# A new issue table for the first sixth of a written-out schedule, and a new origin for the array's first fill

## The chip, the cores and the metric

The kernel runs on one core of a Trainium2 chip. The metric is device time in microseconds; lower is better. Three runs of the kernel before took 366.05, 366.97 and 367.13 us; the median is 366.97 us. One further execution was profiled: it took 365.49 us in all, and its recorded span is 363.7 us.

## The reference, cut to what matters

The first half is a linear attention with a decaying state, for 4 batches, 8 heads, 768 steps and a head dimension of 48:

```python
for t in range(S):
    cur = einsum('bhd,bhe->bhde', u * kt, vt)
    y[:, :, t] = einsum('bhd,bhde->bhe', rt, state + cur)
    state = wt[..., None] * state + einsum('bhd,bhe->bhde', kt, vt)
```

The heads of y side by side give x, of shape (4, 768, 384). The second half is a gated network on it, all in float32:

```python
h = maximum(x @ w_in, 0)                     # 384 -> 1024
u, v = h[..., :512], h[..., 512:]
v_n = (v - mean(v)) / sqrt(var(v) + 1e-6)
v_s = einsum('ts,bsd->btd', w_spatial, v_n) + b_spatial
out = (u * v_s) @ w_out                      # 512 -> 384
```

## The kernel before, in words

**Tiling.** Time is cut in 24 slots of 128 steps (6 per batch). A slot loads its decays W, its keys and queries kr and its values v (L386 to L391), and DVE and POOL prepare them: products of neighbouring decays (L442), a step of k and r by single decays (L446), a scan backwards into F (L449), the floor of its end products (L451) and their reciprocal (L453), a scan forwards into E (L454), and k times F (L456), r times E (L460). TensorE then makes the scores paw (L525), the transposed keys KT (L543), the state's increments (L616) and the outputs py (L560). DVE masks the scores into AS (L529) and adds the increments into S (L629, L631). In the first six slots the bonus term with u goes over TensorE: rk (L414) times up_sb, a small copy of u, gives pg (L419), and bv (L491) is v times pg. The output y is evacuated on ACT and DVE (L663, L665), transposed (yt, L669) and split in a high and a low part (L673 to L679), since each large product is three matmuls of such parts (L686 to L688).

**The network.** hv_unit makes the v half (ph), its sum and sum of squares on ACT (L715 to L718). After every third slot a row of operations on 128x3 tiles named st (L735 to L743) makes mean and scale; L751 or L753 normalizes, L756 and L758 split into vh and vl. g_unit (pu, pv) and out_unit (po) follow for each half batch. The weights are taken in as 64-bit words and turned into float32 parts by integer operations (L354 to L361); the tiles d and e are named after the weight, ('wv', 0) being the first third of the v half of w_in. The spatial weights are split at L329 and L331.

**What sets the order.** Every operation is recorded with the engines it may run on, what it reads and writes, and its buffers. The string PLAN has one word for each of the 1930 operations: a letter for the engine (T is TensorE, V is DVE, A is ACT, G is POOL, S is SyncE's DMA queue) and a number in base 36, a start in hundredths of a microsecond. The operations are sorted by that number and issued:

```python
o.on, o.start = w[0], int(w[1:], 36) / 100
return sorted(self.ops, key=lambda o: o.start)
```

The number is used for the order alone (and for the fills below): each engine works through its own list in order, and an instruction starts when its semaphores allow it.

**Fills.** The function fill walks through the sorted list and, up to the slot FILL_TO, puts matmuls of a zero tile (zk, L893) in front of a TensorE operation wherever the table leaves over 0.3 us before it. How many is reckoned from a time t at which the array is taken to be free; up to COLD each is counted as 0.43 us, after it as 0.224 us. One fill is two records in the trace. TensorE runs them in order like everything else.

Of the kernel before, what the change touches and what calls it, by code (L numbers as in the profile page):

```python
# [18 lines left out]
G = H // 2  # L19
# [12 lines left out]
T2s S4g Tgq Aji Ajc S4x5 S5kl S6o Apg Vrs Vt1 Vxn Azp G12f Spf A1ph V1tz V1wl V1zy A221 G24f Sa0 A134 V15y  # L32
V178 V1al A1co V1kw S28 S3c S8w Vib Tkh Vbe Vk0 Vky Vcx Gf4 Vfy Vgm Vmu Goq A115 A14p Vcc Vzc Ts1 V11e Toz Ar1
T13o T15x Tx1 V10n A15e V1ej T18f A19v V1h2 T1s5 A1vc T1xl A23h Suq A1we V21n V2bl V2g0 A2qc G2xa Sng A1mu
V1r1 V1sa V1uw A2gd V2i8 S1h0 A2kw V2n4 V2pq V2sq A2us V345 S2v6 A3to G496 S238 A3gn V439 S25r A34s V38c S3xz
A4i8 V4r1 S4c7 A5nh V5qb S4ux A5gg V5ms S2sw A5tl G5yv S5jh A5uq V61n S1i4 A2o6 V2rf S5v7 A67e V6i0 S4jx A5af
V5hp S4y9 A5l7 V6jc S1je A2yj V31r V32u V363 A3d0 V5co S2i5 A3ju V3m4 V3q7 V4h2 A53l V5j1 S2qm A3m6 V4gb V4pq
V504 A5k2 V5o3 S4it V4wy V4zd V51f V55w A5mc V5rn T27w T29t T2e2 A2hs A2jk A2mh S5k S7s Sgo Vur Tyf Vlw Vwp
V1ca Vov Vwg V137 V13w Gzk G1f3 A1un A1ty Gfo V1d8 T1ke V1p8 A1fo T12s A1ax T1ov T1vv T1fr V1j8 A1kc V22l T1ym
A20y V23b T26n A28i T2bq A2ct T2j2 T2lj T2o5 A2t0 A2w8 A2wv Smc Sbd S1es V18w T1lv G1dh V1ml V1jy V1fd G1i1  # L40
V1iv V1nj G1o1 V1ya A29k A2a9 V24n T256 V2da A24j T1r9 A1sr T2c7 T2fz T23t V288 A2dv V302 T2ho A2ju V2ll T2ng
A2pa T2qv A2ry T2ts T2vp T2xm A305 A35x A36k A3bf G3xh V3lw G3x1 G3y9 G3z1 G3zt V40i V41z A457 V4cq A41g A43s
V45n A4aq A4e4 G4im S1do S1fw S224 V28y T2rc G22t G2di V2an V25z V27z V2f3 V2jw G2k5 V2o1 A343 A3aq V2x1 T39s
V3cs A388 T31e A32w T2zj T3jt T382 V3c1 A3e5 V3l0 T3l7 A3py V3s9 T3ur A3w1 T3yq A40e T44m T473 T490 A4cp A4fj
A4jd S1pg S210 S2j9 V2vd T3b9 V2uf V30t V37e V2yd V35u V39n V3ac G39w G3ed A3ut A3hs V3n7 T3i1 V3tl A3ng T3h5
A3in T3vf T41u T3ml V3rj G3ss V3ve T438 A46m V484 T4cs A4ft T4k1 A4l4 T4mp T4pa T4r7 A4ud A4w5 A4wt S2g8 S2lb
S3mk V3hf T3nz G3cr V3j3 V3k2 V3em G3l8 V3mu V3oj G3n3 G3u3 A4a1 V41h V3wv T40d V49f V40q T3qz A3sh T4ax T4dh
T3z7 V47c V4bz T4f7 A4h7 V4io T4ly A4n8 T4ot A4pw T4t4 T4v1 T4wy A4zh A51a A51x A54q V585 V55o G57g V58o V597
G59w V5av V5e0 A5hl V5l3 A5ei A5pt V5tc V5bf A5d2 V5fa T5nq S3rn A47o S4aj A4qy S4tt A56b S596 A5r8 T32a T33q
T36m A3by T5fy T5hy T5je T62h T65d T66t V69k V6ce A6ju G6m7 T356 T3e9 T3fp A3l4 T5ku T5ma T5o0 T5pg T5wo T5y4  # L50
V606 V658 A69o V6gp T3rv T3tb T3xa A3zc T63x T689 T69p T6fi T6l9 T6mp V6or V6qe A6s4 G6ui T4gl T4il T4ki A4tb
T5qw T5sc T5ts T5v8 T5zk T610 V63x V66k A68j V6kn T6rx T6td T6z5 T7aw V7cy S7fg T6w9 T6xp T7cc T7ds A7fu S8gi
T760 T780 T79g T7f8 A7ha S7tx T4yv T50b T537 A559 T6gx T6id T6jt T6o5 T6qh T6ut V6zd G73k A78b V7kw T51r T54n
T563 A58o T7go T7l0 T7mg T7pc T7sy T7ud V7wf V7y2 A89o V8ex T58f T59v T5bb A5j0 T85j T88w T8ac T8d8 T8eo T8g4
V8i6 G8k0 A8my V8pf T6b5 T6cl T6e1 A6g3 T7i4 T7jk T7nw T7rh T7vt T7x9 V7ze V84e A863 V87o T8hk T8j0 T8ro T8t4
A8v6 S945 T8bs T8q7 T8uk T8w0 A8y2 S931 T954 T9b5 T9cl T9e1 A9g3 S9hn S38s S3sr S5u3 S43x G47k V4fd V4ef V4k0
G4p2 V4sc V4t1 G4m7 V52r G683 V6b3 V6dq A6l8 A59q A6fn A6kz A6fe A6h5 A6ug T5eh V6xk T57k V59e V577 T70l T5cr
V5gy V5kc V5pf T72b A73r V759 T7qs A7t0 T87j A88m T8kg T8md T8oa A8qt A935 A93s S3lg S45b S6fh S4w1 G4v8 G4sl
# [60 lines left out]
Tqkl Tqrt Tqt9 Aqvb Sqwv Vn8u Tnlb Vp1v  # L119
"""  # L120

GAP, FILL_TO, COLD = 0.3, 5, 7.0

EARLY = 8

# [95 lines left out]
def kernel(  # L221
# [33 lines left out]
    op = prog.op  # L255
# [148 lines left out]
    def slot_prep(i):  # L404
# [490 lines left out]
    def fill(order):  # L895
        t = free = 1.1
# [152 lines left out]
```

## Time and profile before

| | |
|---|---|
| median of three runs | 366.97 us |
| profiled execution | 365.49 us |
| its span | 363.7 us |
| TensorE busy | 354.7 us (98%) |
| DVE busy | 279.1 us (77%) |
| ACT busy | 211.3 us (58%) |
| POOL busy | 138.0 us (38%) |
| loaded and stored by DMA | 47.81 MB |

The shares are means over the whole span. The first 65 us hold the preparation of the weights and the first six slots, the rest runs batch after batch; a share of one stretch is read from the view by stretches.

### The profile page before, as it was taken

How to read it: one execution, taken by the hardware profiler on the slowest of the kernel's cores; microseconds unless marked ns; L12 is line 12 of the kernel's file. 1: busy time of each engine (PE TensorE's matmuls, PEld its weight loads, DVE VectorE, ACT ScalarE, POOL GpSimd, SP SyncE). 2: the span in 40 equal slices, each digit the busy share in tenths (PEclk: the TensorE clock that was granted, in tenths of full speed). 3: DMA queues.
4: the chain of work that ended last, by engine and by line, in shares of the span. 5: the costliest groups of instructions: out<-in, count | busy, mean ns of one | idle time of the engine just before them, and what ended most of it. 6: DMA issues, size and time to landing. Idle time of an engine off the chain costs nothing.

```text
span 363.7 us, 11366 instructions
## 1 busy us (share of the span) xinstructions
PE 354.7 (98%) x4666; PEld 327.9 (90%) x4666; DVE 279.1 (77%) x591; ACT 211.3 (58%) x585; POOL 138.0 (38%) x182
## 2 busy tenths in 40 slices
PE   7998989999999999999999999999999999999997
PEld 6886787899998889799999999999999898899997
DVE  7999998798789998887999865878896876234330
ACT  2478887894555657773645588762464747621212
POOL 3344353412641755615632747132223514013220
DMA  7998546763265365731465445513463331000101
GB/s 205 287 275 231 158 115 174 223 201 98 75 183 167 95 189 179 199 99 43 122 181 166 129 135 162 159 45 112 120 184 96 124 120 45 0 23 0 49 20 69
DMA packets 21546, 47.81 MB, mean 131 GB/s; under 512 B 2545, under 2 KB 10354, under 8 KB 21490
## 3 DMA queue, kind: packets, MB, share of 16 engines
q1 hardware_dynamic: 21346, 46.85, 43.7%
q8 instruction: 37, 0.61, 0.7%
q10 hardware_dynamic: 144, 0.20, 0.1%
q14 instruction: 19, 0.16, 0.1%
HBM read 42.32 MB, written 4.72 MB: 129 GB/s over the span
## 4 chain that ended last, share of the span: by engine, by line
PE 78%; DVE 10%; ACT 6%; issue 2%; DMA 1%; POOL 1%; SPq 0%; DVEq 0%; ACTq 0%; POOLq 0%
PE pv L686 9%; PE pv L688 9%; PE pv L687 9%; PE py L560 5%; PE po L686 5%; PE po L687 4%; PE po L688 4%; PE ph L686 4%; PE ph L688 4%; PE ph L687 4%; PE pu L686 3%; PE pu L688 3%; PE pu L687 3%; PE py L893 3%; PE paw L525 2%
## 5 line engine op out<-in xcount | busy, mean ns | idle before, releaser
L686 PE MATMUL pv<-ws,vh 128*128 128x384 f32 x192 | 65.7, 342 | 0.3 <-ACT us L783 0.2
L688 PE MATMUL pv<-ws,vl 128*128 128x384 f32 x192 | 64.4, 335 | 0.0
L687 PE MATMUL pv<-ws,vh 128*128 128x384 f32 x192 | 64.3, 335 | 0.0
L792 DVE TENSOR_TENSOR t<-pv,b_sb 128x384 f32<-128x384 f32 x32 | 17.6, 552 | 26.7 <-PE pv L688 26.6
L686 PEld LDWEIGHTS pv<-ws,vh 128*128 128x128 f32 x192 | 36.0, 188 | 1.4 <-ACT us L783 0.9
L796 ACT CAST gh<-t 128x384 fp32r<-128x384 f32 x32 | 15.9, 512 | 36.7 <-DVE t L794 25.4
L687 PEld LDWEIGHTS pv<-ws,vh 128*128 128x128 f32 x192 | 36.1, 188 | 0.0
L688 PEld LDWEIGHTS pv<-ws,vl 128*128 128x128 f32 x192 | 36.0, 188 | 0.0
L686 PE MATMUL pu<-xT,wi 128*128 128x384 f32 x96 | 34.2, 357 | 0.0
L686 PE MATMUL po<-wo,gh 128*128 128x384 f32 x96 | 33.1, 345 | 0.0
L688 PE MATMUL pu<-xT,wi 128*128 128x384 f32 x96 | 32.5, 338 | 0.1
L687 PE MATMUL pu<-xT,wi 128*128 128x384 f32 x96 | 32.3, 336 | 0.0
L687 PE MATMUL po<-wo,gh 128*128 128x384 f32 x96 | 32.3, 336 | 0.0
L688 PE MATMUL po<-wo,gl 128*128 128x384 f32 x96 | 32.2, 335 | 0.0
L686 PE MATMUL ph<-wi,xT 128*128 128x512 f32 x72 | 30.6, 425 | 0.3 <-DVE t L792 0.3
L688 PE MATMUL ph<-wi,xT 128*128 128x512 f32 x72 | 28.5, 396 | 0.1
L687 PE MATMUL ph<-wi,xT 128*128 128x512 f32 x72 | 28.3, 393 | 0.0
L505 ACT ACTIVATE AS<-id,dgs 128x64 f32<-128x64 f32 x76 | 20.1, 337 | 6.1 <-DVE dgs L497 6.1
L456 POOL TENSOR_TENSOR kr<-kr,F 112x496 f32<-112x496 f32 x13 | 16.1, 1237 | 15.6 <-DVE kr L446 7.1
L446 POOL TENSOR_TENSOR kr<-kr,W 112x256 f32<-112x256 f32 x16 | 16.4, 1026 | 14.4 <-DMA kr<-in_tr_dram 11.5
L460 POOL TENSOR_TENSOR kr<-kr,E 112x512 f32<-112x512 f32 x13 | 16.2, 1245 | 14.0 <-DVE kr L446 5.8
L794 POOL TENSOR_TENSOR t<-t,us 128x384 f32<-128x384 f32 x9 | 9.6, 1067 | 31.1 <-DVE t L792 29.5
(199 smaller groups left out, 969.4 us busy)
## 6 DMA issues: line engine op xcount, KB each, us to landing
kr<-in_tr_dram SPq DMA_DIRECT2D x24, 448.0 KB, 5.1
N<-in_nat_dram SPq DMA_DIRECT2D x18, 384.0 KB, 3.4
Nw<-in_gt_dram SPq DMA_DIRECT2D x16, 384.0 KB, 3.6
W<-in_tr_dram SPq DMA_DIRECT2D x24, 225.8 KB, 3.5
v<-in_nat_dram SPq DMA_DIRECT2D x24, 192.0 KB, 4.1
out_dram<-ot SPq DMA_DIRECT2D x18, 192.0 KB, 3.1
wst<-in_w_spT_dram SPq DMA_DIRECT2D x12, 192.0 KB, 4.2
out_dram<-ot SPq DMA_DIRECT2D x10, 96.0 KB, 3.5
```

Source lines behind the costliest of these rows:

```text
L446: op({"G": 0.9, "V": dve(half)}, lambda e, n=n: e.tensor_tensor(two(kr()[:, n])[:, :, :, n], two(kr()[:, n])[:, :, :, n], w_()[:, :, :, 1 ...
L456: op({"V": 0.68, "G": 1.07}, lambda e: e.tensor_tensor(seg(kr()[:, 0])[:, :, :L2 - 1], seg(kr()[:, 0])[:, :, :L2 - 1], F()[:, :, 1:].unsqu ...
L460: op({"V": 0.69, "G": 1.1}, lambda e: e.tensor_tensor(seg(kr()[:, 1]), seg(kr()[:, 1]), E().unsqueeze(3).broadcast_to([R, SUB * G, L2, 2]) ...
L505: e.mul(As()[:, j, g, :], id64, dgs()[:, j, g:g + 1])
L560: nc.tensor.matmul(py()[row][L * a:L * (a + 1), D * n:D * (n + 1)], x, z, start=(a, row) not in started, stop=not left[0], skip_group_chec ...
L686: nc.tensor.matmul(ps, ah, bh, start=first, stop=False)
L687: nc.tensor.matmul(ps, ah, bl, start=False, stop=False)
L688: nc.tensor.matmul(ps, al, bh, start=False, stop=last)
L792: op({"V": dve(HT)}, lambda: nc.vector.tensor_tensor(t1(), pv()[:, :HT], b_sb[:, tsl], ALU.add), r=[(pv, 0), ("b", 0)], w=[(t1, 0)])
L794: op({"V": dve(HT), "G": pool(HT)}, lambda e: e.tensor_tensor(t1(), t1(), us(), ALU.mult), r=[(us, 0)], w=[(t1, 0)], port=True)
L796: op({"A": act(HT)}, lambda: nc.scalar.copy(gh(), t1()), r=[(t1, 0)], w=[(gh, 0)])
L893: nc.tensor.matmul(pw, zk, zk, start=False, stop=True, skip_group_check=True)
```

## The change

The operations, buffers and dependencies stay. PLAN is another one: behind the first 70 us of the table all operations stand in the same order as before, with smaller numbers; within it most move, and 30 operations change their engine (19 to DVE from ACT or POOL, 10 from DVE to ACT or POOL, one from POOL to ACT). The first fill is reckoned from 2.4 instead of 1.1 us and the cheaper count begins at 7.9 instead of 7.0 us. The two prices of one memset in the table's list are new; they only say which engines may run it.

```diff
 PLAN = """
-T2s S4g Tgq Aji Ajc S4x5 S5kl S6o Apg Vrs Vt1 Vxn Azp G12f Spf A1ph V1tz V1wl V1zy A221 G24f Sa0 A134 V15y
...
-GAP, FILL_TO, COLD = 0.3, 5, 7.0
+GAP, FILL_TO, WARM_FROM, COLD = 0.3, 5, 2.4, 7.9
...
             if i < AB:
-                op({"G": 0.5, "V": 0.3}, lambda e: e.memset(As(), 0.0), w=[(As, 0), (As, 1)], port=True)
+                op({"G": 0.52, "V": 0.48}, lambda e: e.memset(As(), 0.0), w=[(As, 0), (As, 1)], port=True)
...
     def fill(order):
-        t = free = 1.1
+        t = free = WARM_FROM
         for o in order:
             if o in held and o.on != "T":
                 free = o.start + o.eng[o.on] + 0.25
```

What this does to the lists of the engines is shown at three places. The first is the head of TensorE's list: py0 and zk are the fills, pu the spread of u that ends in up_sb, pg0, pt0 and paw the first slot's bonus, transposed keys and scores. Before:

```order
L893 MATMUL py0_88<-zk_78 128x128 x12
L935 MATMUL pu__180<-few_97,u_sb_110 48x1 x8
L893 MATMUL py0_88<-zk_78 128x128
L419 MATMUL pg0_195<-up_sb_111,rk0_189 128x2 x4
L893 MATMUL py0_88<-zk_78 128x128 x2
L543 MATMUL pt0_212<-ident_92,kr0_143 128x112 x4
L893 MATMUL py0_88<-zk_78 128x128 x3
L525 MATMUL paw_87<-kr0_143 64x64 x16
L893 MATMUL py0_88<-zk_78 128x128 x5
```

Now:

```order
L893 MATMUL py0_88<-zk_78 128x128 x4
L935 MATMUL pu__164<-few_97,u_sb_110 48x1 x8
L893 MATMUL py0_88<-zk_78 128x128 x5
L419 MATMUL pg0_189<-up_sb_111,rk0_181 128x2 x4
L893 MATMUL py0_88<-zk_78 128x128
L543 MATMUL pt0_203<-ident_92,kr0_146 128x112 x4
L893 MATMUL py0_88<-zk_78 128x128 x8
L570 MATMUL py0_88<-bv0_217,ident_92 128x384
L525 MATMUL paw_87<-kr0_146 64x64 x16
```

The first run of fills is 4 instead of 12, another 5 stand behind the spread, and in place of runs of 2, 3 and 5 there are one of 1 and one of 8; the bonus product (L570) comes ahead of the scores.

The second place is the head of DVE's list, from its first memsets of the table or its first product of decays to the first slot's F (names with 0 belong to the first slot, with 1 to the second; the scans L449 and L454 are printed as scalar_tensor_tensor). Before:

```order
L442 TENSOR_TENSOR W2p_83<-W0_140 112x256
L489 MEMSET AS0_85 128x512
L449 SCALAR_TENSOR_TENSOR F0_160<-zz_80,W2p_83 112x256
L453 RECIPROCAL zz_80<-prod_131 112x8
L454 SCALAR_TENSOR_TENSOR E0_165<-W2p_83,zz_80 112x256
L414 TENSOR_TENSOR rk0_189<-kr0_143 112x512
L446 TENSOR_TENSOR kr0_143<-kr0_143,W0_140 112x256 x2
L442 TENSOR_TENSOR W2p_83<-W1_146 112x256
L456 TENSOR_TENSOR kr0_143<-kr0_143,F0_160 112x8x62
L449 SCALAR_TENSOR_TENSOR F1_208<-zz_80,W2p_83 112x256
```

Now:

```order
L489 MEMSET AS0_85 128x512
L489 MEMSET AS1_86 128x512
L300 COPY id64_105<-ident_92 64x64 x2
L272 MEMSET zz_80 128x8
L319 CAST mask_128<-mneg_102 64x64 x2
L442 TENSOR_TENSOR W2p_83<-W0_140 112x256
L449 SCALAR_TENSOR_TENSOR F0_173<-zz_80,W2p_83 112x256
L451 TENSOR_SCALAR prod_131<-F0_173 112x8
L453 RECIPROCAL zz_80<-prod_131 112x8
L941 COPY up_sb_111<-pu__164 48x4
L454 SCALAR_TENSOR_TENSOR E0_179<-W2p_83,zz_80 112x256
L414 TENSOR_TENSOR rk0_181<-kr0_146 112x512
```

Both memsets of AS stand ahead of L442 (one stood behind it and one on POOL), prod (L451) has come from POOL, half of the copy into up_sb (L941) from ACT; the second slot's L442 no longer stands between L446 and L456.

The third place is POOL's list where the first three chunks' mean and scale are made (st0_0) up to the second chunk of spatial weights. Before:

```order
L643 TENSOR_TENSOR S101_116<-S0_114,prod_131 112x192
L460 TENSOR_TENSOR kr5_641<-kr5_641,E5_912 112x512
L739 TENSOR_TENSOR st0_0_622<-st0_0_622 128x3
L736 TENSOR_SCALAR st0_0_622<-st0_0_622 128x3
L740 TENSOR_TENSOR st0_0_622<-st0_0_622 128x3
L741 TENSOR_SCALAR st0_0_622<-st0_0_622 128x3
L742 TENSOR_TENSOR st0_0_622<-st0_0_622 128x3
L442 TENSOR_TENSOR W2p_83<-W6_761 112x256
L331 TENSOR_TENSOR ws1_125<-wst0_0_682,ws0_124 128x384
```

Now:

```order
L460 TENSOR_TENSOR kr4_534<-kr4_534,E4_754 112x512
L739 TENSOR_TENSOR st0_0_595<-st0_0_595 128x3
L740 TENSOR_TENSOR st0_0_595<-st0_0_595 128x3
L741 TENSOR_SCALAR st0_0_595<-st0_0_595 128x3
L456 TENSOR_TENSOR kr5_625<-kr5_625,F5_797 112x8x62
L743 TENSOR_TENSOR st0_0_595<-st0_0_595 128x3
L331 TENSOR_TENSOR ws1_125<-wst2_0_644,ws0_124 128x384
L460 TENSOR_TENSOR kr5_625<-kr5_625,E5_959 112x512
L643 TENSOR_TENSOR S110_117<-S0_114,prod_131 112x192
```

L736 and L742 have gone to DVE and L743 has come from it; L643 and one L460 no longer stand ahead of the row of st operations, and one L442 has left the stretch for DVE.

In the DMA queue the small load of u now stands ahead of the first kr, and the first load of w_in (d 'wv', 0) ahead of the second slot's W.

## Rows read from the trace of the kernel before

**Rows 1.** The page, busy us of each engine (share of the span, instructions).
```profile
PE 354.7 (98%) x4666; PEld 327.9 (90%) x4666; DVE 279.1 (77%) x591; ACT 211.3 (58%) x585; POOL 138.0 (38%) x182
```

**Rows 2.** Stretches: start:end, length, busy PE, PEld, DVE, ACT, POOL, clock, DMA.
```profile
3.77:64.11 60.34, 56.45 (x998) 47.80 (x997) 56.75 (x114) 42.70 (x116) 25.18 (x29) 1.00 0.75 212
65.26:361.00 295.74, 295.01 (x3655) 277.32 (x3656) 218.86 (x467) 165.80 (x464) 111.03 (x140) 1.00 0.39 115
```

**Rows 3.** Chain of waits, first 66 us: start, us, engine, tile, line.
```profile
2.34 5.49 PE py L893 x24
7.83 0.76 PE pu__180 L935 x16
9.11 1.02 PE pg L419 x8
...
64.49 0.72 ACT ph L718 x2
65.26 0.55 PE yt L669 x3
```

**Rows 4.** Time line of the first microseconds: start, us, engine, line, operation [idle before].
```profile
3.77 0.43 DVE L442 TENSOR_TENSOR W2p<-W 112x256 f32<-112x256 f32 x1 [0.18 <-DMA W<-in_tr_dram]
6.49 0.67 DVE L414 TENSOR_TENSOR rk<-kr 112x512 f32<-112x512 f32 x1
8.04 1.26 POOL L460 TENSOR_TENSOR kr<-kr,E 112x512 f32<-112x512 f32 x1 [1.97 <-DVE kr L446]
8.21 1.62 DVE L456 TENSOR_TENSOR kr<-kr,F 112x496 f32<-112x496 f32 x1
9.87 0.67 ACT L354 ACTIVATE e_('wv', 0)_219<-d_('wv', 0)_148 128x512 f32<-128x512 f32 x1 [0.86 <-DMA d_('wv', 0)_148<-in_w_in_dram]
```

**Rows 5.** DVE's waits from 3.5 to 66 us: who for whom, us, times, longest.
```profile
DVE st L743 <- POOL st L742: 1.2, 1, 1.2
...
DVE S L629 <- PE paw L616: 0.4, 1, 0.4
DVE zz L453 <- POOL prod L451: 0.4, 1, 0.4
```

**Rows 6.** Time line, DVE and POOL where both work, 17 to 58 us.
```profile
17.63 1.34 POOL L442 TENSOR_TENSOR W2p<-W 112x256 f32<-112x256 f32 x1 [1.93 <-DMA W<-in_tr_dram]
18.42 0.84 DVE L446 TENSOR_TENSOR kr<-kr,W 112x256 f32<-112x256 f32 x1
...
37.93 2.05 POOL L361 TENSOR_TENSOR wi<-e_('wu', 0)_471,wi 128x512 fp32r<-128x512 f32 x1 [3.31 <-ACT wi L359]
38.75 1.52 DVE L442 TENSOR_TENSOR W2p<-W 112x256 f32<-112x256 f32 x1
...
56.09 1.52 DVE L743 TENSOR_TENSOR st<-st 128x3 f32<-128x3 f32 x1 [1.21 <-POOL st L742]
```

**Rows 7.** DVE by line, 3.7 to 66 us: count, busy us, mean ns, idle before.
```profile
L449 DVE TENSOR_TENSOR_SCAN F<-zz,W2p 112x256 f32<-112x256 f32 x7 | 4.7, 672 | 0.0
L665 DVE TENSOR_TENSOR y<-y,py 128x384 f32<-128x384 f32 x6 | 3.2, 538 | 0.6 <-ACT y L663 0.6
L758 DVE TENSOR_TENSOR vl<-hv,vh 128x512 fp32r<-128x512 f32 x2 | 1.4, 687 | 0.0
L460 DVE TENSOR_TENSOR kr<-kr,E 112x512 f32<-112x512 f32 x2 | 1.4, 678 | 0.0
L451 DVE TENSOR_SCALAR prod<-F 112x8 f32<-112x8 f32 x3 | 0.5, 165 | 0.0
L489 DVE MEMSET AS<- 128x512 f32 x1 | 0.5, 485 | 0.1
L356 DVE TENSOR_SCALAR e_('wv', 1)_429<-e_('wv', 1)_429 128x512 int32<-128x512 int32 x1 | 0.4, 414 | 0.0
L356 DVE TENSOR_SCALAR e_('wo', 0)_699<-e_('wo', 0)_699 128x384 int32<-128x384 int32 x1 | 0.3, 344 | 0.0
```

**Rows 8.** Time line, one clean L331 on DVE.
```profile
37.68 0.54 DVE L331 TENSOR_TENSOR ws<-wst,ws 128x384 fp32r<-128x384 f32 x1
```

More of the change, by code (lines that the diff above doesn't have):

```diff
@@ L37 @@
[L37 to L46, printed above, removed]
@@ L117 @@
[L117 to L119 removed]
+T2s S3c Tbf Ae1 Vfl S47a S5fs S5k Vmu Vo3 Vpc Vv9 Axc G122 Spf A1qu V1t5 V1vq V1z3 A216 G236 Sa0 A134 V162
+V17y V1d7 A1fa V1xf S28 S4g S7s Vhl Tjr Vbe Vja Vk8 Vcn Veo Vf8 Vfx Vl6 Gs7 A177 Ayr V2s Vrz Tvn V12k Tnb Aot
+Tts T18f Txg V11u A14p V1ew T1a5 A1e8 V1fp T1ht A1jx T1li A1ml S1d2 A25i V2ao V2cj V2hf A2pd G2ry Snu A1kz
@@ new lines @@
+V1n7 V1rf V1u1 A22m V2lq S1w6 A2hv V2ks V2nf V2q1 A2wi V35o S3oi A426 G43v S2gs A38a G4cn S2io A3h0 G3ve S2ky
+A4pg V4rc S4qc A5ip V5lj S4p8 A5bo V5i0 S3ip A5os G5u2 S5eo A5px V5wv S1f9 A3a4 V3cq S5qe A62m V6d8 S4am A565
+V5cx S4t4 A5gf V6ej S1xa A2qs V30e V34c V3gy A4zu V57w S2nl A3jy V3m2 V3qg V3s3 A4y6 V5e9 S2sw V498 V4bo V4ku
+V4p4 A5fa V5jb S3tv A4gp V4ie V4nt V50h A5hk V5mu T1o6 T26y T28v A2bm A2fk A2g7 S6o S8w Smq Vx6 Tzd Vr1 Vyv
+V170 Vta Vwy Vzt V14e V106 G1gr A1j8 A1q5 V3w V1ip T1lz V1oe A1gq T1az A1d1 T1qn T1td T1g4 V1k1 A1nn V1qk T1v3
@@ new lines @@
+A1x3 V20s T22l A24g T261 A2ak T2dw T2gd T2iy A2na A2p3 A321 Slm Sbd S1at V19m T1cf G1f4 V1bb V1c9 V1h1 G1jo
+V1ks V1lg G1k8 G1od A1t4 A1sf V224 T1wh V254 A1y5 T1si A1tz T23x T2as T1xy V26x A282 V2t2 T2ci A2ei V2fz T2ia
+A2jk T2l5 A2m8 T2o2 T2pz T2rw A2xy A2zq A30d A3d3 V3gq V3e1 G3g6 G3kd G3l5 V3lu G3pw A3y3 A45o V49z V3tw A473
+V4go A3sf A402 V4j5 S1bx S1e5 S1ye V281 T2lm G210 V2bl V29p V23f G26l V27o V2e8 G2eg V2j4 A39f A367 V2rq T2wk
+V37c V2w2 T2tt A2vb T2up T3f7 T2yd V31h A33p V3fy T3gx A3ix V3ke T3n5 A3og T3qa A3rd T3th T3ve T3xb A49k A4bc
@@ new lines @@
+A4dy S1zi S20m S2fo V2wt T2zr V2p3 V2zg V2yi V2ts V2vt V315 V328 G31d G396 A37l A36w V395 T3ib V3n5 A3l9 T3eb
+A3ft T3qr T3z8 T3js V3oz A3vl V3yi T40y V42y V44l T46n A48i T4cb A4fm T4h7 T4j4 T4li A4o1 A4rn A4sb S2cz S2ek
+S3hl V3e9 T3nu G37k V3j6 V3i8 V3ah V3ch V3mt V3v6 G3n1 G3y3 V3te A41h V3wv T436 V46o G42b T3sm A3ue T47c T497
+T42c V45x V48h T4ax A4cx V4ee T4g8 A4hz T4l1 A4m4 T4np T4pm T4rj A4u2 A4vv A4wi A4zb V52q V50a G522 V53v V54f
+G554 V563 V597 A5ct V5gb A59p A5l0 V5oj V56m A58a V5ah T5ib S3qy A43b S466 A4j1 S4lw A521 S54w A5mf T32r T347
@@ new lines @@
+T38j A3dm T5aj T5cj T5dz T5x2 T5zy T61e V64r V67m A6ev G6hf T35n T373 T39z A3c1 T5ff T5gv T5il T5k1 T5ra T5sq
+V5us V60g A64w V6bx T3bf T3cv T3l5 A3pi T5yi T62u T64a T6a2 T6fu T6ha V6jc V6l0 A6mp G6p3 T44n T4dc T4es A4ql
+T5lh T5mx T5od T5pt T5u6 T5vm V5z4 V61r A63r V6fv T6mi T6ny T6tr T75h V77j S7a1 T6qu T6sa T76x T78d A7af S8b3
+T70l T72l T741 T79t A7bv S7oi T4tg T4uw T4xt A50z T6bi T6cy T6ee T6iq T6l2 T6pe V6ty G6y5 A72w V7fh T4wd T4z9
+T50p A54e T7b9 T7fl T7h2 T7jy T7nj T7oy V7r0 V7sn A84a V89i T530 T54g T55x A5e8 T805 T83h T84x T87t T899 T8aq
```

141 lines of the change are left out of this document (65 added, 76 removed).

## The prediction, made before the changed kernel was run

> **What bounds the kernel now.** The page says TensorE 98%, DVE 77%, POOL 38% [rows 1]; the reader should not stop there, since the change lives in the first 66 us. So I read the stretches next. From 65.26 to 361 us TensorE is busy 295.01 of 295.74 us [rows 2]: whatever the first stretch gives or costs is handed to the end unchanged, because 0.7 us of idle time is all that could swallow or return it. In the stretch before, from the first product of decays (3.77) to the addition that completes the sixth slot's y (64.11, read off the time line as the start of the last DVE operation that the transpose at 65.26 needs), TensorE's busy share flatters it, for fills stand in its gaps. DVE is busy 56.75 of 60.34 us there, ACT 42.70, POOL 25.18 [rows 2]. The chain of waits starts on 24 fill records from 2.34, goes to the spread at 7.83, and at its end hops through ACT to the transpose at 65.26 [rows 3]. So the reader should see DVE as the engine that sets the pace from 4 to 64 us, with TensorE's fills in the chain at the very beginning and ACT at the very end.
>
> Now split DVE's 60.34 us. 3.6 us are idle. Nine of its instructions last far longer than others of their form, each with a POOL instruction beside it: the first is L456 at 8.21 (1.62 us beside POOL's L460, against 0.68 for the similar L460 on DVE [rows 4, 7]), the last is L743 at 56.09, 1.52 us for a tile of 128x3, where an operation on 112x8 takes 0.165 [rows 6, 7]; L442 takes 1.52 instead of 0.43 beside POOL's L361, L446 0.84 instead of 0.43 [rows 4, 6]. These four lose 0.94 + 1.36 + 1.09 + 0.41 = 3.8 us; the five between them (0.87 to 1.30 us each) lose another 2.3 by the same subtraction. So DVE's stretch is 6.1 us blocked, 3.6 idle and 50.6 plain work: 3.77 + 50.6 + 6.1 + 3.6 = 64.1.
>
> **The change, part by part.** *Fills and spread.* 4 fills (8 records) instead of 12 stand ahead of the spread. At 5.49 / 24 = 0.23 us a record [rows 3] the spread can start at 2.34 + 1.8 = 4.2 instead of 7.8. That is 3.6 us on paper and little on the path: pg also needs rk, which DVE finishes at 7.16 [rows 4], so pg moves from 9.11 to about 7.4, and behind it the transposed keys need k after L456, which ends at 9.83 [rows 4]. What DVE visibly lost to the late array is the 0.4 us before L629, waiting for paw [rows 5]. I take 0.4 for this part; the bounds are 0, if the longer runs of 8 and 10 fills now make the same wait, and 0.4.
>
> *DVE's list up to that last addition.* Sixteen operations come in and eleven go. Those that have a like on the other side cancel (L456 for L460, L442 for L446, one of the two prods, pairs of L643, L753, L480). What is left in: one memset 0.49, one prod 0.17, a copy into up_sb at about the same 0.17, two conversions L355 priced like L356, 0.41 + 0.34, one small st operation 0.17, one evacuation of y 0.54 as L665, one scan 0.67: 2.96 us. Left out: two L331 at 0.54 and one L758 at 0.69: 1.77 [rows 7, 8]. Net +1.2, and since each DVE instruction starts some 0.08 us before its predecessor ends (8.21 against 7.87 + 0.42 shows it), five more instructions weigh 0.4 less: **+0.8 us of work on the bounding engine**. Moving work off ACT and POOL pays nothing by itself; they have room.
>
> *Idle time of DVE.* The wait of 1.2 before L743 is for five st operations on POOL that stood behind L643 and L460 there [rows 5]; now only three are on POOL and neither is ahead of them, but two hops between the engines are added. I take 0.8 of the 1.2 as gone (bounds: none, all). The 0.4 for prod [rows 5] goes, since it is on DVE itself. Against this, L355 on DVE needs the first load of w_in, which landed only at 9.87 before [rows 4]; its load is now ahead of W of the second slot, and where ACT waited 0.86 us alone, DVE, with everything behind it in its list, may wait. I count 0.4, between nothing and 0.9. So idle goes from 3.6 to 3.6 - 0.4 - 0.8 - 0.4 + 0.4 = 2.4, with 1.5 to 3.6 as bounds.
>
> *Blocked time of DVE.* The table gives starts, but nothing holds POOL back to them: L460 on POOL at 8.04 began as soon as DVE's L446 let it [rows 4]. So the overlaps fall where they fall. Before the addition POOL loses four instructions net, about 1.7 of its 25.2 us (one each of 1.07, 0.90, 1.27 and smaller ones go, two L331 and an L460 come), and DVE's own share of operations that were seen blocked shrinks by about 2 us of some 28. Scaled by both, 6.1 x 0.93 x 0.93 = 5.3; L743, the largest single loss, is now on POOL where it can block nobody for long, and I take 5.0. Bounds 3.5 (all the large ones gone) and 6.8 (DVE's denser list is hit more often).
>
> On this place the Trainium skill has a rule, SBUF — State Buffer, section "Who interferes with whom": DVE and GpSimd share one pair of ports, and whoever issues first keeps it for the whole instruction while the other is fully blocked. The rows agree that one blocks the other (1.26 us of POOL end at 9.30, and L456 ends 0.53 later [rows 4]). By that rule the moved L442 matters: L456 now follows L446 directly and would have the ports before L460 on POOL does, so the 0.94 us would go as well and the time would be 0.9 lower than mine. The rows don't promise it: POOL's L442 at 17.63 pushed in between two back-to-back DVE instructions and cost the second 0.4 [rows 6], so the same block may only strike L355 or L356 instead. The sum goes by the rows.
>
> *Sum.* The last addition starts at 3.77 + 50.6 + 0.8 + 2.4 + 5.0 = 62.6 instead of 64.1. (The memsets that now stand before the first product are counted in the work; the place where they run changes nothing.) TensorE and ACT follow: ACT carries about two microseconds less ahead of the transpose, so it is not what holds it. Gain 1.5 us: span 362.2, the profiled execution 364.0. That execution was 365.49, 1.5 below the median 366.97, so the forecast for the median is **365.5 us**.
>
> **Rivals.**
>
> *A: everything is swallowed.* Idle time stays near 3.0 and blocked time at 5.9: 3.77 + 51.4 + 8.9 = 64.1, no change, 367.0. For it: the added 0.8 us is certain, the savings are waits, and a denser list has less idle time to absorb the next block. Against: two of the waits have lost their cause by name.
>
> *B: slower, by POOL on a denser DVE.* One mechanism: POOL's in-order list starts early against the new neighbours on DVE, as at 8.04 and 37.93 [rows 4, 6], and L355 to L358, now side by side on DVE with POOL's L460 and L361, are blocked. With 7.5 blocked and 3.6 idle the addition starts at 66.3, and the end is 2.2 later: 369.2. It decides once blocked and idle time together pass 8.9, and shows beyond 10.0. For it: nine such blocks were there before. Against: POOL has less to do in this stretch.
>
> *C: the waits really go.* Blocked 3.8 (L456 and L743 both clean and one other), idle 1.8: 60.8, a gain of 3.3, 363.7. For it: the new origin of the fills fits the 2.34 of the array [rows 3], the old one did not, so TensorE's operations of the first slots can come up to 1.7 us earlier when DVE is there. Against: of the 6.1 us only L743's 1.36 and perhaps L456's 0.94 have a cause that is seen to go.
>
> *D: the change does not act.* Excluded as a whole, since all lists differ; but the first fills alone could be all that acts, for 0.4 us, and that lies inside A.
>
> **How the numbers follow.** About 0.3% or 1.1 us is what a measurement of this kernel tells from no change. My forecast, a gain of 1.1 to 2.5 us, gets 0.38; C, beyond that, 0.17; A, within 1.1 us, 0.32; B 0.13. Faster 0.55, same 0.32, slower 0.13. The range reaches from 363.2 (C with a little less than its full gain at the far end, about 1 in 14 below) to 368.2 (the near end of B, about 1 in 9 above); the forecast's own range is 364.5 to 365.9.
>
> **What would show it.** In the profile after: the spread near 4.2 and pg before 8; DVE's last addition for the sixth slot between 62 and 63, TensorE dense from about 63.8; no wait of over 0.5 before the st operations; L456 of the first slot at 0.7 (the rule on ports) or 1.6 us; DVE's instructions of over 0.2 us excess adding up to 4 to 5.5 us. I am wrong if TensorE is not dense by 65 although DVE is on time (then ACT or the fills bound), if TensorE waits over 1.5 us in all after that point, or if blocked time on DVE is above 6.5.

## The result, and the profile after

The changed kernel takes 368.68 us (median of five, 368.09 to 372.49) against 366.05 us of the kernel before beside it (364.31 to 367.13): a ratio of 1.0104, 95% interval [1.0063, 1.0145]. It is slower by 1.0%, where 0.4% faster was forecast. The profiled execution took 368.68 us, its span is 366.9. The ratios, here and below, follow the means of the undisturbed executions, so they differ from those of the medians; by the medians the loss is 0.7% or 2.6 us.

First the page's busy times and its row of the granted clock, which the page of before did not have, then two stretches: from 3.77 us, as in [rows 2] (DVE's first product itself stands at 4.71 now, behind the memsets), to the addition that completes slot 5's y, and the dense part behind.

```profile
PE 358.1 (98%) x4660; PEld 331.6 (90%) x4660; DVE 280.2 (76%) x600; ACT 210.4 (57%) x582; POOL 133.6 (36%) x176
...
PEclk9989998999999999999999999999999999999999
```

```profile
3.77:67.94 64.17, 60.33 (x993) 51.74 (x992) 57.27 (x124) 40.68 (x111) 24.50 (x27) 0.95 0.73 210
69.20:364.00 294.80, 293.83 (x3649) 276.42 (x3649) 219.29 (x470) 166.74 (x466) 107.63 (x136) 1.00 0.38 114
```

The last addition starts at 67.94 us, 3.83 later than the 64.11 of [rows 2], and the span is 3.2 longer: the loss is made in the first sixth and handed on. In that sixth DVE is busy 57.27 us, 0.5 more than before, and idle 6.9 in place of 3.6. So the bounding engine didn't get much more work; something made it wait. Its waits from 3 to 68 us, and those of PE to 70 us (who for whom, us in total, times, longest):

```profile
DVE y L663 <- PE py L560: 3.9, 1, 3.9
DVE y L665 <- ACT y L663: 1.0, 1, 1.0
DVE AS L529 <- PE paw L525: 0.5, 1, 0.5
```

```profile
...
PE ph L686 <- DVE bv L491: 2.1, 1, 2.1
PE paw L616 <- issue: 0.7, 1, 0.7
PE py L560 <- issue: 0.5, 1, 0.5
PE pg L419 <- DVE rk L414: 0.4, 1, 0.4
```

None of the three waits that [rows 5] shows is left. The new one is large: DVE waits 3.9 us for PE, which itself has waited 2.1 for DVE. The time line and the chain show the place (start, us, engine, line, tile):

```profile
54.91 0.48 ACT L679 CAST xT<-yt 128x384 fp32r<-128x384 f32 x1 [0.20 <-PE yt L676]
...
54.92 0.55 DVE L357 SCALAR_TENSOR_TENSOR e_('wo', 1)_899<-d_('wo', 1)_665,e_('wo', 1)_899 128x384 int32<-128x384 int32 x1
...
55.36 0.55 PE L543 MATMUL pt<-ident,kr 112*128 112x112 f32 x4
...
56.09 0.25 DVE L480 COPY vs<-v 64x192 f32<-64x192 f32 x1
56.35 0.55 DVE L753 TENSOR_SCALAR hv<-hv,st 128x512 f32<-128x512 f32 x1
...
56.81 0.68 DVE L454 TENSOR_TENSOR_SCAN E<-W2p,zz 112x256 f32<-112x256 f32 x1
...
57.41 0.53 DVE L491 TENSOR_TENSOR bv<-v,pg 128x384 f32<-128x384 f32 x1
...
57.99 0.80 PE L686 MATMUL ph<-wi,xT 128*128 128x512 f32 x1 [2.09 <-DVE bv L491]
```

```profile
57.49 0.46 DVE bv L491
57.95 0.04 issue
57.99 0.80 PE ph L686
58.79 0.43 PE ph L687
59.22 0.43 PE ph L688
...
61.26 0.23 PE ph L687
61.49 0.24 PE ph L688
61.72 1.08 PE py L560 x64
...
66.39 0.52 issue
66.90 0.43 PE py L560 x12
```

Read it backwards. The state matmuls of slot 4 (L560) start at 61.72, behind the nine ph matmuls of slot 3, which the new order puts ahead of them. ph could have started when pt ended, at 55.91, since its inputs were there (L679 ends at 55.39); but it got one of three PSUM buffers that take turns, the one that pg of slot 5 had held, and that is free only when bv of slot 5 has read it, at 57.94. (No data passes from that bv to ph of slot 3; the buffer is the tie that is left.) In DVE's new list bv stands behind L357, L358, L480, L753 and the scan L454. PE stands still for 2.09 us, and then seven ph matmuls take 0.33 to 0.80 us where the last two take 0.23: about 1.4 us more. In the old order these stood as follows:

```profile
54.35 0.54 DVE L491 TENSOR_TENSOR bv<-v,pg 128x384 f32<-128x384 f32 x1
...
54.94 0.55 PE L669 MATMUL yt<-ident,y 128*128 128x128 f32 x3 [1.31 <-DVE bv L491]
...
58.75 0.50 PE L686 MATMUL ph<-wi,xT 128*128 128x512 f32 x1
```

So PE waited for this bv before, too: 1.31 us, ahead of yt, with the matmuls behind it at full pace (the second ph starts 0.34 us after the first, the later ones 0.23 to 0.24 apart). In the new order the wait is 0.8 us longer, it stands ahead of ph and, behind ph, of the state matmuls that DVE waits for, and a slower clock follows it. PE's stretches show that second part (start:end, length, busy (count), granted clock, DMA):

```profile
20.00:25.00 5.00, 3.93 (x57) 0.85 0.71 201
25.00:30.00 5.00, 5.00 (x91) 0.81 0.49 125
...
55.00:60.00 5.00, 2.91 (x11) 0.76 0.73 225
60.00:65.00 5.00, 5.00 (x126) 0.90 0.87 272
```

Before, the row said 1.00 (2.4 GHz) all through [rows 2]; here it falls, after PE stood still, to the lower level (0.50, 1.2 GHz) for a part of each of these stretches. A warning on this row: it also says 1.00 where the trace has no record of the clock. The trace of before has none at all, that of the changed kernel its first at 13.24 us. Ahead of that the length of like matmuls must be read: a fill takes 0.23 to 0.26 us a record until 7.8 us before and until 12.9 in the changed kernel, and about 0.12 later on. So the array also came to its full pace later.

### The profile page after: what moved, and what is told of

Same layout as the page of the kernel before. It is cut to its first block, busy times and chain, and to the rows that moved or that the text cites. A ratio compares the mean times of both kernels' runs of the same rounds, so it can differ in the third digit from the quotient of the medians.

```text
span 366.9 us, 11365 instructions
## 1 busy us (share of the span) xinstructions
PE 358.1 (98%) x4660; PEld 331.6 (90%) x4660; DVE 280.2 (76%) x600; ACT 210.4 (57%) x582; POOL 133.6 (36%) x176
## 4 chain that ended last, share of the span: by engine, by line
PE 79%; DVE 10%; ACT 5%; DMA 3%; issue 2%; DVEq 0%; ACTq 0%
PE pv L686 9%; PE pv L688 9%; PE pv L687 9%; PE py L560 6%; PE ph L686 5%; PE po L686 5%; PE ph L688 4%; PE po L687 4%; PE ph L687 4%; PE po L688 4%; PE pu L686 3%; PE pu L688 3%; PE pu L687 3%; PE paw L525 2%; PE yt L669 2%
## 5 line engine op out<-in xcount | busy, mean ns | idle before, releaser
L686 PE MATMUL ph<-wi,xT 128*128 128x512 f32 x72 | 31.0, 431 | 2.4 <-DVE bv L491 2.1
L688 PE MATMUL ph<-wi,xT 128*128 128x512 f32 x72 | 28.9, 402 | 0.0
L687 PE MATMUL ph<-wi,xT 128*128 128x512 f32 x72 | 28.7, 399 | 0.0
L460 POOL TENSOR_TENSOR kr<-kr,E 112x512 f32<-112x512 f32 x14 | 19.2, 1371 | 21.9 <-DVE kr L446 10.8
L529 DVE COPY_PREDICATED AS<-mask,paw 128x512 f32<-128x512 int32 x24 | 17.7, 738 | 4.9 <-POOL AS L507 3.4
L641 ACT ACTIVATE S<-S,prod 112x48 f32<-112x48 f32 x76 | 19.1, 323 | 3.6 <-DVE S L629 1.9
```

The costliest lines, as they stand in the source:

```text
L460: op({"V": 0.69, "G": 1.1}, lambda e: e.tensor_tensor(seg(kr()[:, 1]), seg(kr()[:, 1]), E().unsqueeze(3).broadcast_to([R, SUB * G, L2, 2]) ...
L529: op({"V": 0.735}, lambda: nc.vector.copy_predicated(As(), mask.unsqueeze(1).unsqueeze(1).broadcast_to([P, 2, G, L]), pa()[:, :, :G * L].r ...
L641: e.mul(S1[i % 2][a][:, g, :], S0[:, g, :], Wc[:, g:g + 1])
L686: nc.tensor.matmul(ps, ah, bh, start=first, stop=False)
L687: nc.tensor.matmul(ps, ah, bl, start=False, stop=False)
L688: nc.tensor.matmul(ps, al, bh, start=False, stop=last)
```

## The experiments

Theory 1: one late evacuation (bv of slot 5) stops PE for 2.1 us and costs the clock for another 1.4. Theory 2: many small losses before 50 us add up. Theory 3: the clock alone. Theory 4 came later. Each kernel ran beside the kernel before on the same chip; times in us, the last column is where slot 5's y is added in the profiled execution.

| kernel | median (lowest to highest, n) | before | ratio, 95% interval | y of slot 5 |
|---|---|---|---|---|
| changed | 368.68 (368.09-372.49, 5) | 366.05 | 1.0104 [1.0063, 1.0145] | 67.94 |
| e1_fill_origin | 367.10 (366.24-367.45, 10) | 365.63 | 1.0046 [1.0029, 1.0064] | 66.40 |
| e2_bv5_early | 366.01 (364.46-369.27, 12) | 365.63 | 1.0030 [1.0000, 1.0061] | 65.93 |
| e3_memsets_back | 367.69 (365.43-370.78, 8) | 365.63 | 1.0067 [1.0033, 1.0102] | 67.77 |
| e4_fill_cap | 370.14 (366.34-372.04, 6) | 365.63 | 1.0105 [1.0060, 1.0150] | 68.47 |
| e5_keep_warm | 367.63 (366.17-371.51, 12) | 365.88 | 1.0061 [1.0031, 1.0092] | 68.88 |
| e6_bv5_and_fills | 365.43 (363.59-368.76, 12) | 365.88 | 1.0005 [0.9976, 1.0034] | 63.37 |
| e7_all_three | 366.73 (363.62-368.84, 12) | 365.88 | 1.0023 [0.9992, 1.0054] | 66.55 |
| e8_table_alone | 369.21 (367.71-373.05, 6) | 365.88 | 1.0113 [1.0058, 1.0168] | 69.28 |
| e9_shift | 366.11 (365.06-367.56, 12) | 365.56 | 1.0012 [0.9989, 1.0036] | 65.44 |
| e10_shift_only | 369.09 (366.48-369.88, 6) | 365.56 | 1.0089 [1.0057, 1.0122] | 66.45 |
| e11_all_shift | 366.07 (365.35-367.03, 12) | 365.56 | 1.0015 [1.0000, 1.0030] | 64.91 |
| e12_early_packet | 364.83 (363.76-369.20, 12) | 365.75 | 0.9993 [0.9965, 1.0022] | 68.43 |
| e13_packet_first | 372.43 (367.69-374.11, 6) | 365.68 | 1.0119 [1.0070, 1.0168] | - |

**e2: the late bv alone.** One word of the table, bv of slot 5 from 50.71 to 47.95, which puts it behind L631 on DVE:

```diff
-A41h V3wv T436
+A41h V3p7 T436
```

> The changed kernel with one DVE instruction moved: bv of slot 5 (L491), which frees the third PSUM buffer of its kind, stands directly behind the S subtraction of slot 4 (L631, 54.66 us) instead of behind two L357/L358 steps, the vs copy, the L753 step and the E scan (57.41 us). Theory 1 (one late evacuation: PE waits 2.1 us for it at 55.91 to 57.99, its clock falls, and the next ph matmuls take 0.43 us instead of 0.23): the wait of PE on bv is under 0.3 us, the granted clock of 55 to 65 us is back near 1.00, y of slot 5 is added about 3 us earlier than 67.94, and the kernel takes 365.2 to 366.3 us, no different from before. Theory 2 (many small losses before 50 us: memsets first, POOL's blocks, long runs of fills): the moved bv gives under 1.0 us, 367.7 us or more.

The wait on bv is gone, and PE's stretches where it stood read:

```profile
55.00:60.00 5.00, 5.00 (x34) 1.00 0.56 179
60.00:65.00 5.00, 4.98 (x179) 1.00 0.78 249
```

The ratio falls from 1.0104 to 1.0030, by 0.74% or 2.7 us, and the intervals don't meet: theory 1 holds for most of the loss, and its sum of 3.5 was 0.8 too high. (By the medians the gain is 2.3 us.) It isn't all: 0.3% stays, and three of the twelve executions lie near 369 us. e9 and e10 below, run side by side, differ by this bv and five fills, and their intervals (1.0012 and 1.0089) don't meet either.

**e5: the wait stays, PE works in it.** Nine fills ahead of ph.

```diff
-            if o.on == "T":
-                b = max(t, free)
+            if o.on == "T": warm(9 * (o.n == 289)); b = max(t, free)
+            if o.on == "T":
```

> The changed kernel with nine fills put ahead of the ph matmul that waits 2.09 us for bv of slot 5: the wait stays, only PE does not stand still in it. If the clock's fall after the wait is a cost of its own (theory 1 puts 1.4 us on it: seven ph matmuls of 0.43 us in place of 0.23), the granted clock of 55 to 65 us is back near 1.00, those matmuls take about 0.23 us again, and the kernel takes 367.0 to 367.6 us. If the wait alone decides, it stays at 368.2 to 369.2 us.

The chain behind bv is now (start, us, what):

```profile
61.11 0.50 PE ph L686
61.62 0.24 PE ph L687
61.85 0.23 PE ph L688
62.09 0.24 PE ph L686
```

The clock stays at 1.00 there and the matmuls take 0.23 us. The ratio falls by 0.43% or 1.6 us, near what was expected, but the intervals overlap, so the size is only likely. What the lower clock does to these matmuls is shown by the rows. That the fills are what kept it is not shown: in e10's profiled execution (366.48, the fastest of its six) PE stands still for the same 2.10 us with no fills in the wait, and the nine ph matmuls still take 0.23 us each behind the first. So the wait alone doesn't bring the slower clock each time, and how the 2.7 us divide between the two stays open.

**e3 and e4: the early losses.** e3 puts AS0's memset behind the first product on DVE and AS1's on POOL (`V2s` to `Vby`, `V3w` to `Gfo`); e4 holds later runs of fills to three.

```diff
-  warm(max(0.0, cold - 0.1) / 0.43 + max(0.0, o.start - max(b, COLD) - 0.1) / 0.224)
+  warm(min(99 if b < COLD else 3, max(0.0, cold - 0.1) / 0.43 + max(0.0, o.start - max(b, COLD) - 0.1) / 0.224))
```

> The changed kernel with the two memsets of AS back where they were before: AS0 on VectorE behind the first W2p multiplication, AS1 on GpSimd. Theory 2: DVE starts its chain at 3.8 instead of 4.71 us, and 0.65 to 0.94 us of that reach the end: 367.7 to 368.1 us. Theory 1: the start is made up for by 43 us, where the changed kernel stood within 0.8 us of before, and the wait for bv near 56 us stays: 368.2 to 369.2 us.

> The changed kernel with runs of fills after the first us held to 3 (the runs of 8 and 10 that PE was still working through when bv of slot 0 at 12.34 us and AS0 at 17.23 us were ready, and that of 4 at 24.20). Theory 2: the state matmuls of slot 0 start at about 17.3 instead of 18.99 us, and over 1 us of that reaches the end: 366 to 367.6 us. Theory 1: the start is not what decides, 368.2 to 369.5 us, and the PE wait for bv near 56 us stays. Theory 3 (TensorE's clock alone): with fewer fills the granted clock of 20 to 30 us (0.85 and 0.81 now) is lower still and the kernel is slower, 369 us or more.

e3's ratio is 0.37% or 1.3 us lower, as theory 2 has it, but the intervals overlap; the wait for bv is 2.1 us in both kernels. e9 and e11 below differ by the memsets alone and are equal (366.11 and 366.07), so their place is worth nothing that shows. In e4 the state matmuls of slot 0 came 1.6 us earlier (17.41 against 18.99), and nothing came of it: PE then stood still for 1.35 and 0.66 us near 20.4 and 22.5, the granted clock of 20 to 30 us fell to 0.72 and 0.60, and the ratio is that of the changed kernel (the median, 370.14, is higher, as theory 3 has it; in the profiled execution PE also stood still for 2.04 us at 232.5 to 234.5, for nothing that the profile shows). An earlier start and a worse clock act against each other in e4, so it doesn't separate theories 2 and 3. What sets theory 2 aside as the main cause is e2: one word of the table, for a place near 56 us, gave back most of the loss with the early part as it was. Theory 3 falls with it as a cause apart from that wait.

**e1 and e8: the two halves of the change.** e1 is the old table with the new counting of fills, e8 the new table with the old counting.

```diff
-GAP, FILL_TO, COLD = 0.3, 5, 7.0
+GAP, FILL_TO, WARM_FROM, COLD = 0.3, 5, 2.4, 7.9
...
-        t = free = 1.1
+        t = free = WARM_FROM
```

> The kernel before with its old table, and of the change only the new counting of the fills (three fills fewer ahead of the spread, 9 instead of 12). Both theories below put the loss into the table, so both expect no measurable difference from before: 365.0 to 367.0 us, the spread about 0.7 us earlier than 7.83 and pg no earlier than 8.2, because it also waits for DVE's rk at 7.16. If it were slower by over 0.3%, the counting of the fills would be a cause of its own.

> The changed kernel with the fills counted as before (three more ahead of the spread), so the new table alone. By theory 1 the loss sits in the table near 56 us: 368.2 to 369.5 us, as the changed kernel, with the wait for bv there. If the new counting of the fills is what costs (the old table with the new counting was slower by 0.46%, with a granted clock of 0.50 at 10 to 15 us), this is faster than the changed kernel by 1 us or more: 367.5 us or less.

e8 equals the changed kernel, with the wait for bv in it: the table carries that loss under either counting. (It isn't a clean copy: its clock is 0.50 at 10 to 15 us.) e1 is a miss of both theories: under the old table the new counting costs 0.46% by itself. With 9 fills for 12, PE stands idle for 0.87 us before pt of slot 0 at 9.95, and its granted clock is 0.50 from 10 to 15 us, where the fills of before are at full pace from 10.2 on. Under the new table the row says 1.00 there, but it has no record before 13.24, and by the fills the array is at the lower pace until 12.9.

**e6 and e7: fills where PE stood still.** With the moved bv, two fills ahead of pg and three ahead of the L616 at 22.80; e7 has e3's memsets as well.

```diff
+            if o.on == "T": warm({200: 2, 179: 3}.get(o.n, 0)); b = max(t, free)
```

> The changed kernel with bv of slot 5 moved forward as in e2_bv5_early, and two and three fills ahead of the matmuls before which PE stood still at 20.67 to 21.09 and 22.15 to 22.80 us. If those two stops cause the half-speed stretch of 23.4 to 26.7 us, that stretch is gone (granted clock of 20 to 30 us at 1.00 in place of 0.85 and 0.81), and if it costs time at the end the kernel takes 0.5 to 1.5 us less than e2_bv5_early's 366.0, and its slow executions near 369 us are gone: 364.5 to 365.5 us. If DVE alone sets the pace there, the clock comes back and the time does not: 365.6 to 366.4 us.

> The changed kernel with all that helped so far: bv of slot 5 forward, the two memsets of AS back, and the fills ahead of the two stops near 21 and 22.5 us. If the single gains (2.7 us and 1.3 us by the ratios to before) add up: 364.0 to 365.0 us, no slower than before and perhaps faster. If both act on the same lateness of DVE ahead of 60 us, no better than the better one: 365.5 to 366.5 us.

The clock comes back (20 to 30 us of e6):

```profile
20.00:25.00 5.00, 4.81 (x66) 1.00 0.84 246
25.00:30.00 5.00, 5.00 (x171) 1.00 0.36 84
```

(e6's trace has no record of the clock; its fills at 22.0 to 24.6 us follow each other by 0.11 to 0.12 us, at full pace.) e6's profiled execution took 363.59 us with y of slot 5 at 63.37, 0.74 earlier than in before's profiled one. That isn't a gain shown: it is the fastest of twelve, and the fastest of before beside it took 363.58. The median, 365.43, is in the expected range and no different from before, but two executions still lie at 368 to 369, which were to go. e7 was to reach 364.0 to 365.0 if the single gains added up; they don't: 366.73. It was profiled at 368.84, and what stands out beside e6 is one row: in e7 PE stands still for 1.64 us in the middle of slot 1's state matmuls, for nothing that the profile shows, and the clock falls behind it (0.66 at 30 to 35 us).

**e9 to e13: packets of instructions.** Theory 4: the trace has a queue of kind "instruction", whose packets of 16,384 bytes come one for every 127 matmul records of PE (one record and its weight load each). That these are PE's instructions is inferred from that count and from where PE stops. In the first 70 us of the profiled executions PE's unexplained stops inside a run of like matmuls lie at its records 346, 473 and 981 (one of 0.2 us at 220), and each ends 1.3 to 1.7 us after such a packet has landed; e4's at 234.5 us, 23 times 127 records behind record 346 to within two, does so too (1.57). The stretch looked at is from record 219 to 346, counted from the records and packets of each trace:

| kernel | record 219 at | packet | record 346 at | PE stops there |
|---|---|---|---|---|
| before | 20.39 | 22.40 to 23.52 | 27.24 | no |
| changed | 22.91 | 27.57 to 28.69 | 30.06 | no (1.36 behind the packet) |
| e6 | 21.68 | 22.15 to 23.15 | 28.37 | no |
| e2 | 22.95 | 28.57 to 29.65 | 30.96 | 0.90 |
| e7 | 21.36 | 27.39 to 28.38 | 29.70 | 1.64 |
| e8 | 21.91 | 28.02 to 29.10 | 30.56 | 1.46 |
| e5 | 23.37 | 29.45 to 30.52 | 31.87 | 2.57 |
| e12 | 21.44 | 30.11 to 31.20 | 32.52 | 2.67 |

From 19.7 to 21.6 us SP issues five loads of 1.6 MB in all in the changed kernel; keys for slot 3, the fourth of them, land at 29.06. In these traces the packet goes ahead of the large ones or waits until they have nearly landed. e9 (on e6), e10 (on the changed kernel) and e11 (on e7) pass record 219 earlier in the program by 24 records:

```diff
-            nc.tensor.matmul(pw, zk, zk, start=False, stop=True, skip_group_check=True)
+            nc.tensor.matmul(pw[:, :C >> half], zk, zk[:, :C >> half], start=False, stop=True, skip_group_check=True)
```

> As e6_bv5_and_fills, and the ten fills ahead of slot 0's state matmuls are replaced by 22 of half the width: about the same time on PE, but 24 more matmul records. Reason: in the profiled executions so far PE stands still, for nothing that the profile shows, only in front of its matmul records 346, 473 and 981 (127 or a multiple of it apart), each time 1.3 to 1.7 us after a packet of the instruction queue (16,384 bytes) has landed, and that packet starts 0.5 to 6.1 us after PE has passed the record 127 earlier, late where loads are in flight. Theory 4 (the scatter of the executions between 363.6 and 369 us comes from this packet's place among the loads of 20.4 to 28 us): record 219 is now passed near 20.0 us, ahead of those loads, the packet starts before 22 us, PE does not stop at record 346, and the executions near 368 to 369 us are gone: median 364.3 to 365.2 us, highest under 367.5. Rival: the scatter comes from the clock or from DVE, and the median stays at 365.4 with executions up to 368.8 us.

> The changed kernel with only the 22 half-wide fills in place of the ten. Theory 1 (the wait for bv near 56 us decides): 367.0 to 368.5 us, since that wait and the clock's fall behind it stay; theory 4 adds that the executions above 371 us are gone. If the instruction packet were most of the loss, 365.5 to 366.5 us.

> As e7_all_three, and the 22 half-wide fills in place of the ten. Theory 4: the lead of e6_bv5_and_fills over e7_all_three (1.3 us between the medians, 363.59 against 368.84 us in the profiled executions) was the instruction packet alone (no stop at record 346 in the first, 1.64 us in the second); with the packet early it is gone and this is as fast as e9_shift or up to 0.6 us faster: 363.9 to 365.0 us. If the memsets' old place is itself a loss beside the moved bv, it stays 0.5 to 1.3 us above e9_shift.

The packet started 0.61 and 0.48 us behind record 219 in e9 and e11, PE did not stop at record 346, and the spread of twelve executions shrank from 5.2 us in e6 and e7 to 2.5 and 1.7, with none above 367.6. That is as theory 4 has it, but not by the way it meant: record 219 was passed at 22.23 and 21.95, not near 20.0, and the large loads were issued only from 24.19 and 23.78 on. The time is not: the medians, 366.11 and 366.07, lie above both forecasts, and the lowest rose from 363.6 to 365.1, because a fill of half the width takes as long as a whole one (44 records in 5.1 us), so slot 0's state matmuls came 2.8 us later. e10 keeps the wait for bv (2.10 us) and most of the loss, as theory 1 expects, though its median is above the 367.0 to 368.5 forecast. e12 tries the same with small matmuls (64x48).

```diff
+            if o.on == "T": warm({200: 2, 179: 3, 51: 4}.get(o.n, 0)); warm(16 * (o.n == 51), 64, 48); b = max(t, free)
```

> As e6_bv5_and_fills, and the ten fills ahead of slot 0's state matmuls are now four fills and sixteen small ones (64x48): 20 more matmul records than before the edit, and this time no more time on PE (a record of half the width took 0.116 us in e9_shift, as much as a whole one, so that edit cost 2.6 us of PE; a 64x48 record is estimated at 0.02 to 0.06 us from the 64 records in 1.15 us of the state matmuls). Theory 4: record 219 is passed at about 19.6 to 20.2 us, its packet starts before 21 us, PE does not stop at record 346, and the slow executions are gone without e9_shift's price: median 364.2 to 365.2 us, highest under 367.2, against 365.6 of before. Rival: what keeps the median at 366 in e9_shift and e11_all_shift is not the longer fills but DVE's or ACT's lateness, then 365.6 to 366.4 us.

It has the lowest median of all, 364.83, but isn't distinguishable from before, and three of twelve took 368 us or more. The profiled execution is one of these, at 368.99 us. It passed record 219 at 21.44, not 20, yet just ahead of the five loads (issued from 21.46 to 23.26), and its packet came last all the same. First the stop inside a run of like matmuls, then the DMA queues from 30.1 to 31.3 us, when hardly anything but this packet was under way:

```profile
29.62 0.23 PE L560 MATMUL py<-v,AS 64*64 64x48 f32 x2
...
32.52 0.26 PE L560 MATMUL py<-vs,AS 64*64 64x48 f32 x2 [2.67 <-issue]
```

```profile
q8 instruction: 1, 0.02, 5.7%
q1 hardware_dynamic: 4, 0.00, 1.4%
```

Something else differs in it: the sixteen fill records from 10.96 us take 3.65 us, and also in e5, where they take 3.05 in the changed kernel, the same program up to there, and 2.87 in e6. So in some executions the array comes to its full pace later. For the scatter of the times this is a rival of the packet, and no run separates the two.

e13 replaces most fills of the first 20 us by small ones, to pass the record before the loads.

```diff
+            if o.on == "T": warm({200: 2, 179: 3, 51: 3}.get(o.n, 0)); warm({50: 20, 51: 13}.get(o.n, 0), 64, 48); b = max(t, free)
```

> As e12_early_packet, but PE passes record 219 before the loads of 19.6 to 22 us are issued: the eight fills ahead of bv's transposition are 20 small ones (64x48) and the ten ahead of slot 0's state matmuls are three fills and thirteen small ones, 36 records more than e6_bv5_and_fills in about the same time (a small record took about 0.067 us in e12_early_packet, a whole one 0.116). Theory 4: record 219 is passed near 18.5 us, its packet starts before the loads' packets, PE does not stop at record 346 in any execution, and the slow ones of e12_early_packet (368.0, 369.0 and 369.2 of twelve) are gone: median 364.0 to 364.8 us, highest under 367 us; before stands at 365.7. If executions at 368 to 369 us are still there and the packet is early, the scatter has another cause. If small fills hold the clock less well, the granted clock of 10 to 20 us falls below 1.00 and the median rises to 366 us or more.

It failed much as the last sentence has it. In the profiled execution, at 374.11 the slowest of the six, PE's own matmuls took twice as long behind the small fills until about 35 us (bv's transposition 1.65 us in place of 0.81). The row of the granted clock says 1.00 there, but the trace has no record of it before 36.55. Record 219 was passed at 25.57, not 18.5, its packet started 0.28 us later, there was no stop at those records, and the six executions took 367.7 to 374.1 us all the same. So a stop behind a packet that landed late is seen at record 346 in five traces (e2, e5, e7, e8, e12). That these stops make the executions of 368 us and more is argued, from e7 and e12 and from their absence in e9 and e11, and not shown: e2's execution has two stops of 0.90 and 0.95 us and took 366.68, and e13's has none. A kernel that has the early packet for nothing was not found, and what decides whether the packet goes ahead of the loads (e6 and e7 pass the record 0.3 us apart, e12 ahead of all five) stays open. No version is shown to beat the kernel before.

## Why the prediction was wrong, step by step

- **Fills and spread.** The spread came at 4.35 (4.2 forecast), pg at 7.95 (7.4). pg then took 1.84 us where it had taken 1.02 [rows 3], so it ended at 9.79 against 10.13: little was gained. The array had not come to its full pace (fills at 0.25 us a record until 12.9), which the sum had not looked at. Priced at 0.4, worth near 0, in the bounds.
- **DVE's work and its blocked time: close.** Busy 57.27 us against 50.6 + 0.8 + 5.0 = 56.4. The blocked share, summed as in the prediction over the instructions with excess, is 5.6 us, in the bounds of 3.5 to 6.8. That the memsets' place changes nothing was wrong at the spot (DVE's first product at 4.71, not 3.77), but without effect that shows at the end (e9, e11).
- **The port rule.** By the Trainium skill (SBUF — State Buffer, "Who interferes with whom") whoever issues first keeps the shared ports. The trace agrees: L456 started 0.16 us ahead of POOL's L460 and took 0.67 us in place of the 1.62 of [rows 4]. The saving did not stay; not the next DVE instruction (L355 at 9.10, 0.42 us) but the one after it, L356, still beside that L460, took 1.26 us for 0.41, as the prediction had said it might:

```profile
8.52 0.67 DVE L456 TENSOR_TENSOR kr<-kr,F 112x496 f32<-112x496 f32 x1
8.68 1.85 POOL L460 TENSOR_TENSOR kr<-kr,E 112x512 f32<-112x512 f32 x1 [6.62 <-DVE kr L446]
...
9.56 1.26 DVE L356 TENSOR_SCALAR e_('wv', 0)_200<-e_('wv', 0)_200 128x512 int32<-128x512 int32 x1
```

- **DVE's idle time: the step that failed.** "So idle goes from 3.6 to 2.4, with 1.5 to 3.6 as bounds": it went to 6.9. The waits that were to go went (before L743, for prod, for paw before L629), and the feared one for the load of w_in did not come. But the sum took old waits away and, but for that load, put the new ones at nothing without a reason; it never asked what the moved PE instructions would wait for. One wait of 3.9 us for PE stands there now. The new order pulls ph of slot 3 ahead of slot 4's state matmuls and leaves bv, which frees its PSUM buffer, behind five DVE instructions. Both lists, the count of three buffers, and the 1.31 us that PE waited for this bv before were there to be read. This one wait, with the slower clock that mostly follows it, is 2.7 of the 3.8 us lost by the ratios (0.74 of 1.04%). The cause of the rest stays open; candidates are the clock's fall at 23 to 27 us, PE's unexplained stops and the array's later full pace. e6, which has no fall at 23 to 27 us, is not slower than before.
- **Passing it on: right in kind.** PE is busy 293.83 of 294.80 us behind 69.2, and 3.2 of the 3.83 us reach the end.
- **The rivals.** B named the right side and almost the time, 369.2 us, by luck: its reason, more blocking, did not come (DVE was blocked for 5.6 us, 6.1 before). C's 363.7 was seen only as the fastest execution of e6, and before has one as fast.

## What to carry to other kernels

When an order moves a matmul forward, look up which instruction frees its PSUM buffer and where that stands in the other engine's list: a shorter list of old waits says nothing about new ones. A wait of the matmul engine can cost a slower clock behind it besides its own length: here it did in the changed kernel and not in e10. With fills in the wait the matmuls behind it ran at full pace (e5, e6). When one program's executions lie some 5 us apart, look for stops without a releaser at the same instruction numbers, and at what the DMA queues carried just before; and don't take the fastest execution of one kernel for a gain over the median of another.

## What the runs showed that was not expected

- The traces show DMA packets of kind "instruction", of 16,384 bytes, one for 127 matmul records of PE, and PE stopped for up to 2.67 us (e12) when one came late behind loads.
- A fill of 64 columns took 0.116 us a record, as much as one of 128; one of 64x48 about 0.06 (e12).
- With small fills for whole ones (e13, one execution) the matmuls took twice as long for some 20 us although the row of the granted clock says 1.00; the same holds for pg's 1.84 us in the changed kernel. In both places the trace has no record of the clock, and the row says 1.00 for want of one. There a matmul's duration beside its like tells more than the row.
